# A planned state-space-plus-MLP kernel: raising the rank of the near chunks' exponential, multiplication and mask, with a new draw for the planner

## The chip, the cores and the metric

The kernel runs on one core of a Trainium2 chip. The core has a matrix engine (PE, with its weight loads shown apart as PEld), a vector engine (DVE), an activation engine (ACT), a general engine (POOL) and SP, which issues nearly all DMAs. Each engine works through its own list of instructions in order; semaphores make an instruction wait for another engine or for a DMA. The metric is the device time of one execution in microseconds (us). The kernel before takes 322.32 us (median of 3 runs, 321.84 to 322.35).

## The reference, cut to what matters

```python
# a: (4, 8, 768); x: (4, 8, 768, 32); B, C: (4, 8, 768, 16); chunks of 32 in time
log_a = np.log(np.clip(a, 1e-06, 1.0))
for c in range(nc):
    cum = np.cumsum(la, axis=-1)
    L = np.exp(cum[:, :, :, None] - cum[:, :, None, :])      # decay from j to i
    L = L * causal                                            # i >= j
    M = np.einsum('bhin,bhjn->bhij', Cc, Bc) * L
    y[:, :, sl] = M @ x + (C @ state) * exp(cum)              # written out with einsum
    state = decay_full * state + sum_j decay_from_j * B_j x_j
x = y.transpose(0, 2, 1, 3).reshape(3072, 256)
h = x @ w_in                                                  # 256 x 2048
g = h - np.tanh(h)
return g @ w_out                                              # 2048 x 256
```

A scan over time with a decay for each head comes first; its output feeds a two-layer network with 2048 inner features and `g = h - tanh(h)` between the layers. Both weight matrices arrive as float64.

## The kernel before, in words

**Scan.** The kernel uses chunks of 112 time steps, not 32: 28 chunks, numbered so that the same chunk of the four batches stands together. The 16 rows of state of a batch are put beside the 112 rows of inputs, so that one product of 128 rows does both parts of `y`. For each chunk `ck` there are these steps, whose line numbers are those of the profile:

- the product of B and C (`att`, written on PE), and the decays `exp(cum_i - cum_j)` (`lt`);
- their product with each other on DVE, the causal mask by POOL (`cut`, L547), and then `y` on PE (`y`), which is the masked matrix times x. For chunks that hand a state on, PE also computes the new state (L659 or, for the first pairs of chunks, `z`, L587), and ACT copies it into the top rows of a later x (L593, L665).

The decays are made in three ways. `first_tile` makes chunks 0 to 3: POOL masks a log, PE sums it up (`cp`, L465 and L467), ACT takes the exponential (L482), DVE multiplies (L486). `chunk_a` makes the **near chunks**, 4 to 9: PE makes the sums beside the product of B and C in one `att` buffer (L522, L527), ACT takes the exponential of 128x896 elements (L531), DVE multiplies (L535), POOL masks. `chunk_l` makes the chunks from 10 on: a DMA spreads the sums over the partitions (L560), ACT adds a bias and takes the exponential in eight parts (L565), POOL masks, and `crossed` multiplies on DVE (L699) with an `att` that PE makes for two chunks at once (`cross`, L693). There is one `att` buffer (four banks of PSUM): the next `att` waits until DVE has multiplied with the last. Chunks from 10 on go through PE in pairs (`pair_y`, L719).

**Weights.** `conv(u)` turns a piece `u` of 256 inner features from float64 words (`raw`, loaded by SP at L312, 512 KB for each half: half 0 for the first layer, half 1 for the second) into float32: ACT converts the high words (L341), DVE shifts, clamps and joins bits (L346, L351, L354, L361), and then ACT rounds to the short format (`wh`, L365) and DVE takes the rest (`wl`, L368). Pieces 0 and 1 are done in halves of 128x512 elements, and their plain float32 words are used at once by the first tile (L772 and, from `wf`, L849).

**Network.** The 3072 rows are cut into tiles, four of 256 and four of 512; the four narrow ones are later swept in two pairs, called tiles 8 and 9. For a tile `t` and feature `f`, PE makes `ph{t}_{f}` (L777, three products each of rounded parts and rests; L772 plain), ACT the tanh (L809), DVE the difference `g` (L813), then ACT and DVE split it (`gh` L817, `gl` L823), and PE multiplies by the second layer into `o{t}` (L859, or L849 for pieces 0 and 1 and the narrow tiles). The first sweep covers narrow tiles 0 to 3 with features 0 to 3; a result of it, `o0` to `o3`, is moved away by ACT (L888). The buffers for `ph` are two, and `cp` and the pairs' `y` use the same two. The buffers `po0` and `po1` are one each: `z`, the single chunks' `y` and `o` take turns in them, so that `z1` cannot start before ACT has copied `z0` away.

**What sets the order.** Nothing is issued as it is written. Each step is handed to `op(...)` with its engine, a cost in us and what it reads and writes, and `Order` plans all of them: a list schedule in which an engine, when it is free, takes the ready step of best rank. The rank of a step is its start in a backward schedule, less its `urge`, plus a random number between -0.3 and 0.3:

```python
prio = [-rstart[i] - self.ops[i][1] - self.urge[i] + self.JITTER * rng.uniform(-1, 1) for i in range(n)]
```

A lower number goes first. `search` does 16 rounds from one `SEED` and keeps the plan with the shortest end by its own costs; its order is then issued on all engines, SP included. `URGE` is 3.0 (us). In the kernel before it is given to the steps of `first_tile` for the first tile's chunks (L497, L499, L502) and to the copies of their `y` (L679).

## Time and profile before

| | |
|---|---|
| median of 3 runs | 322.32 us |
| profiled execution, its own time | 322.54 us |
| its span, first to last instruction | 320.8 us |
| what lies around the span | 1.7 us |
| PE busy | 313.0 us, 98% |
| DVE busy | 216.8 us, 68% |
| ACT busy | 210.0 us, 65% |
| POOL busy | 64.1 us, 20% |
| granted PE clock | 0.999 |

A row of a timeline gives the start from the span's beginning and the time taken, then the engine, the line, the operation, and what is written and read; in square brackets stands the idle time of the engine just before it and what ended it. A row of waits gives who waited for what, and the total, the number and the longest in us. Busy times of PE overlap, since a matmul starts before the one ahead has drained; the distance between two starts on PE tells its pace.

### The profile page before, as it was taken

What the parts mean: (1) busy time and instruction counts of PE and PEld (TensorE: products, weight loads), DVE (VectorE), ACT (ScalarE), POOL (GpSimd) and SP (SyncE); (2) the same over time, 40 slices, a digit from 0 to 9 for tenths busy, and PEclk for the clock granted to TensorE, in tenths of its full rate; (3) what the DMA queues carried; (4) which work ended last, traced back from release to release, by engine and by line L of the source; (5) the groups of instructions that cost most, each with busy time, mean ns of one, the idle gap of its engine ahead of it and who ended that gap; (6) DMA issues with size and microseconds to landing.
All of it is one profiled execution on the core that took longest, in us unless ns stands there. A gap on an engine that the chain in (4) does not pass through costs nothing.

```text
span 320.8 us, 5650 instructions
## 1 busy us (share of the span) xinstructions
PE 313.0 (98%) x2112; PEld 251.3 (78%) x2112; DVE 216.8 (68%) x314; ACT 210.0 (65%) x471; POOL 64.1 (20%) x94
## 2 busy tenths in 40 slices
PE   8898999999999999999999999999999999999995
PEld 6466888788888877787878878878878788888883
DVE  7999987798889856558474764574755745645551
ACT  6668888476789679767584773965847744544451
POOL 6525544002223223212120220201101100000000
PEclk9999999999999999999999999999999999999999
DMA  6766686148923256471506005007500000100001
GB/s 199 238 205 251 182 289 252 51 161 246 309 44 66 44 152 160 67 223 38 188 0 225 0 0 210 0 1 233 205 21 0 0 2 0 66 2 0 0 0 65
DMA packets 15450, 35.25 MB, mean 110 GB/s; under 512 B 2464, under 2 KB 4416, under 8 KB 15424
## 3 DMA queue, kind: packets, MB, share of 16 engines
q1 hardware_dynamic: 13696, 31.76, 29.6%
q0 software_dynamic: 1728, 3.15, 5.7%
q8 instruction: 16, 0.26, 0.3%
q14 instruction: 10, 0.08, 0.1%
HBM read 28.32 MB, written 3.43 MB: 99 GB/s over the span
## 4 chain that ended last, share of the span: by engine, by line
PE 89%; DVE 7%; ACT 2%; issue 1%; DVEq 0%; ACTq 0%
PE ph L777 39%; PE o L859 37%; PE o L849 4%; PE y L719 3%; PE att L693 3%; ACT lt L565 1%; DVE lt L486 1%; PE warm L1018 1%; PE y L652 1%; DVE wv L351 1%; DVE wm L354 1%; DVE wm L346 1%; DVE lt L535 1%; DVE wv L361 1%; PE att L527 1%
## 5 line engine op out<-in xcount | busy, mean ns | idle before, releaser
L813 DVE TENSOR_TENSOR g<-ph,g 128x512 f32<-128x512 f32 x96 | 65.9, 687 | 45.7 <-ACT g L809 45.6
L809 ACT ACTIVATE g<-ph 128x512 f32<-128x512 f32 x96 | 57.4, 598 | 56.3 <-PE ph L777 55.3
L823 DVE TENSOR_TENSOR gl<-g,gh 128x512 fp32r<-128x512 f32 x88 | 65.1, 742 | 38.5 <-ACT gh L817 37.3
L777 PE MATMUL ph<-xh,wh 128*128 128x512 f32 (+1 forms) x200 | 75.6, 382 | 0.0
L777 PE MATMUL ph<-xh,wl 128*128 128x512 f32 (+1 forms) x200 | 74.5, 377 | 0.0
L817 ACT CAST gh<-g 128x512 fp32r<-128x512 f32 x88 | 54.3, 618 | 25.6 <-DVE g L813 24.7
L859 PE MATMUL o<-gh,wh 128*128 128x512 f32 x176 | 69.2, 393 | 0.0
L859 PE MATMUL o<-gl,wh 128*128 128x512 f32 x176 | 68.7, 390 | 0.0
L859 PE MATMUL o<-gh,wl 128*128 128x512 f32 x176 | 68.5, 389 | 0.0
L777 PE MATMUL ph<-xl,wh 128*128 128x512 f32 (+1 forms) x200 | 58.0, 376 | 0.0
L547 POOL TENSOR_SCALAR_AFFINE_SELECT lt<-lt 128x896 f32<-128x896 f32 (+1 forms) x24 | 26.8, 1118 | 119.7 <-ACT lt L565 111.6
L777 PEld LDWEIGHTS ph<-xh,wh 128*128 128x128 f32 x200 | 37.6, 188 | 7.8 <-issue 0.7
L777 PEld LDWEIGHTS ph<-xh,wl 128*128 128x128 f32 x200 | 37.6, 188 | 6.8
L777 PEld LDWEIGHTS ph<-xl,wh 128*128 128x128 f32 x200 | 36.3, 188 | 7.0
L565 ACT ACTIVATE lt<-lt,ncum 128x112 f32<-128x112 f32 (+1 forms) x144 | 41.6, 374 | 0.0
L859 PEld LDWEIGHTS o<-gh,wh 128*128 128x128 f32 x176 | 33.0, 188 | 7.7 <-issue 0.8
L859 PEld LDWEIGHTS o<-gl,wh 128*128 128x128 f32 x176 | 33.0, 188 | 7.4 <-DVE gl L823 0.5
L859 PEld LDWEIGHTS o<-gh,wl 128*128 128x128 f32 x176 | 33.0, 188 | 6.7
L904 POOL DMA_DIRECT2D pt<-part x12 | 10.7, 972 | 50.8 <-ACT part L901 50.5
L699 DVE TENSOR_TENSOR lt<-att,lt 128x896 f32<-128x896 f32 (+1 forms) x18 | 18.9, 1050 | 0.0
L849 PE MATMUL o<-g,wf 128*128 128x256 f32 x64 | 15.4, 387 | 0.3 <-DVE g L813 0.3
L849 PEld LDWEIGHTS o<-g,wf 128*128 128x128 f32 x64 | 11.7, 189 | 2.7 <-issue 0.6
(97 smaller groups left out, 266.6 us busy)
## 6 DMA issues: line engine op xcount, KB each, us to landing
lt<-cumr SPq DMA_DIRECT2D x18, 512.0 KB
raw<-w_d SPq DMA_DIRECT2D x16, 512.0 KB
bc<-bc_d SPq DMA_DIRECT2D x14, 352.0 KB
x<-x_d SPq DMA_DIRECT2D x14, 256.0 KB
pt<-part POOLq DMA_DIRECT2D x12, 256.0 KB, 4.1
out_d<-ob SPq DMA_DIRECT2D x8, 256.0 KB
braw<-bn_d SPq DMA_DIRECT2D x14, 112.0 KB
out_d<-pt SPq DMA_DIRECT2D x4, 256.0 KB
```

What stands on the lines that cost most here:

```text
L547: nc.gpsimd.affine_select(out=k["l"][:, :, 0:q], in_=k["l"][:, :, 0:q], pattern=[[0, H], [1, q]], compare_op=ALU.is_ge, fill=0.0, base=N, ...
L565: nc.scalar.activation(k["l"][:, h, 0:q], k["l"][:, h, 0:q], AF.Exp, bias=ncum[:, h, ck : ck + 1])
L693: nc.tensor.matmul(out=a_[:, i], lhsT=bb[r], rhs=cc[r, :, 0 : qlen(ck)], start=True, stop=True)
L699: nc.vector.tensor_tensor(out=l, in0=chs[j]["a"], in1=l, op=ALU.mult)
L777: nc.tensor.matmul(out=ph[:, i * w : i * w + w], lhsT=w_[:, u, 0, k, j * P : (j + 1) * P], rhs=(xh, xl)[p][:, k, ts], start=p == i == k == ...
L809: nc.scalar.activation(g[:, 0:used], gs[t, f][0][:, 0:used], AF.Tanh)
L813: nc.vector.tensor_tensor(out=g, in0=ph, in1=g, op=ALU.subtract)
L817: nc.scalar.copy(gh[:, 0:used], gs[t, f][1][:, 0:used])
L823: nc.vector.tensor_tensor(out=gl[:, 0:used], in0=g[:, 0:used], in1=gh[:, 0:used].bitcast(F32), op=ALU.subtract)
L849: nc.tensor.matmul(out=po[t, seg][e], lhsT=wf[:, u, 256 * j + e * P : 256 * j + (e + 1) * P], rhs=gs[t, f][1][:, i * w : i * w + w], start ...
L859: nc.tensor.matmul(out=po[t, seg][e], lhsT=w_[:, u, 1, j, e * P : (e + 1) * P], rhs=g[:, i * w : i * w + w], start=f == seg[0] and k == 0 ...
L904: op("POOL-", 1.0, lambda e=e: nc.gpsimd.dma_start(out=pts[m][:, e], in_=obs[t, e], accum_op=ALU.add), r=[name, n_pt[2 * m], n_pt[2 * m + ...
```

## The change

Three calls in `chunk_a` (the exponential, the multiplication, the mask of chunks 4 to 9) and the mask of the chunks from 10 on get `urge=URGE`: their rank is improved by 3 us in the plan. The seed of the random part becomes 252 instead of 537. No instruction is added, taken away or altered; the costs that the planner works with are the same.

```diff
-    ROUNDS, JITTER, SEED, EARLY, LOOK = 16, 0.3, 537, 8.0, 0.5
+    ROUNDS, JITTER, SEED, EARLY, LOOK = 16, 0.3, 252, 8.0, 0.5
@@ chunk_a
-        op("ACT", 0.92, fn_e, r=[n_a], w=n_l)
-        op("DVE", 1.08, fn_m, r=[n_a], w=n_l)
-        op("POOL", 0.97, lambda: cut(ck), w=n_l)
+        op("ACT", 0.92, fn_e, r=[n_a], w=n_l, urge=URGE)
+        op("DVE", 1.08, fn_m, r=[n_a], w=n_l, urge=URGE)
+        op("POOL", 0.97, lambda: cut(ck), w=n_l, urge=URGE)
@@ chunk_l
-        op("POOL", 0.97, lambda: cut(ck), w=n_l)
+        op("POOL", 0.97, lambda: cut(ck), w=n_l, urge=URGE)
```

What comes of it is a new order on every engine. In the rows below a name carries the chunk, piece or tile first and a running number last (`wv1_352` is piece 1).

**The loads of weight piece 1, on SP.** Before, from the write-out of the sums (`cum3`) on, up to the second half of `raw1`:

```order
L1067 DMA cum3_115<-parts_111 112x3x128 x2
L312 DMA raw1_208<-w_d 128x1024
L281 DMA bc2_213<-bc_d 128x704
L1072 DMA lt_c_112<-cum3_115 6x1x768
L1074 DMA rt_c_113<-cum3_115 3x2x768
L1072 DMA lt_c_112<-cum3_115 6x1x768
L1074 DMA rt_c_113<-cum3_115 3x2x768
L1072 DMA lt_c_112<-cum3_115 6x1x768
```

Now, from the second of the loads of `rt_c` on:

```order
L1074 DMA rt_c_113<-cum3_115 3x2x768
L1072 DMA lt_c_112<-cum3_115 6x1x768
L1074 DMA rt_c_113<-cum3_115 3x2x768
L1072 DMA lt_c_112<-cum3_115 6x1x768
L1074 DMA rt_c_113<-cum3_115 3x2x768
L312 DMA raw1_284<-w_d 128x1024 x2
L293 DMA x2_348<-x_d 128x512
L302 DMA braw1_107<-bn_d 112x256
```

The first half of `raw1` stood ahead of the eight loads of `lt_c` and `rt_c`, which can only start when the sums have been written out; now both halves stand behind them. (The second half of piece 0 and `bc1`, which stood ahead of the write-out, now stand right behind it.)

**From `att4` to the second feature of tile 0.** On ACT, now, from chunk 4's exponential on:

```order
L531 ACTIVATE lt4_340<-att4_319 128x8x112
L620 CAST xh_91<-y3_331 128x2x112
L341 ACTIVATE wv1_352<-raw1_284 128x512
L632 CAST xh_91<-xf_93 128x2x336
L341 ACTIVATE wv1_352<-raw1_284 128x512
L531 ACTIVATE lt5_389<-att5_358 128x8x112
L593 COPY x2_348<-z0_372 16x2x64 x4
L809 ACTIVATE g0_0_403<-ph0_0_342 128x512
```

On PE, before:

```order
L527 MATMUL att4_343<-bc2_213 128x224 x4
L772 MATMUL ph0_0_354<-xf_93,wv0_192 128x256 x4
L587 MATMUL z0_369<-x0_151,bw0_338 16x32 x16
L772 MATMUL ph0_2_388<-xf_93,wv1_264 128x256 x4
L522 LDWEIGHTS lt_c_112
```

On PE, now:

```order
L522 MATMUL att5_358<-rt_c_113,lt_c_112 128x224
L527 MATMUL att5_358<-bc2_233 128x224 x4
L587 MATMUL z0_372<-x0_164,bw0_218 16x32 x16
L587 MATMUL z1_406<-x1_212,bw1_393 16x32 x16
L772 MATMUL ph0_2_427<-xf_93,wv1_352 128x256 x4
```

`ph0_2` moved from before `att5` and `z1` to behind both; on ACT the copies of `z0` (L593), for which `z1` waits, moved behind both conversions of piece 1 and behind chunk 5's exponential.

**From chunk 7's `y` to `att12`.** On ACT, before, from the rounding of weight piece 2 (`wh`) to the first far exponential, of chunk 10:

```order
L365 CAST wh_89<-wv2_489 128x1024
L620 CAST xh_91<-y7_633 128x2x112
L665 COPY x5_539<-y7_633 16x64 x4
L809 ACTIVATE g2_0_683<-ph2_0_651 128x512
L531 ACTIVATE lt9_690<-att9_674 128x8x112
L341 ACTIVATE wv3_696<-raw3_563 128x1024
L888 COPY pt0_525<-o1_0_0_619 128x2x256
L665 COPY x6_664<-y8_701 16x64 x2
L620 CAST xh_91<-y8_701 128x2x112
L665 COPY x6_664<-y8_701 16x64 x2
L809 ACTIVATE g2_2_746<-ph2_2_721 128x512
L565 ACTIVATE lt10_694<-lt10_694,ncum_105 128x112 x8
```

On ACT, now, to the exponential of chunk 11 (three copies of `y7`, chunk 9's exponential, the cast of `y7` and its last copy stand just ahead of the first row):

```order
L365 CAST wh_89<-wv2_616 128x1024
L341 ACTIVATE wv3_709<-raw3_614 128x1024
L665 COPY x6_666<-y8_713 16x64
L620 CAST xh_91<-y8_713 128x2x112
L665 COPY x6_666<-y8_713 16x64 x3
L809 ACTIVATE g2_0_739<-ph2_0_669 128x512
L809 ACTIVATE g2_2_742<-ph2_2_690 128x512
L565 ACTIVATE lt10_688<-lt10_688,ncum_105 128x112 x8
L665 COPY x6_666<-y9_754 16x64 x3
L620 CAST xh_91<-y9_754 128x2x112
L665 COPY x6_666<-y9_754 16x64
L565 ACTIVATE lt11_730<-lt11_730,ncum_105 128x112 x8
```

On PE, before, from the end of `ph3_2`:

```order
L777 MATMUL ph3_2_824<-xl_92,wh_89 128x256 x4
L849 MATMUL o3_0_0_848<-g3_0_837,wf_94 128x256 x4
L693 MATMUL att12_857<-bc6_786 128x224 x8
L719 MATMUL y10_866<-lt10_694,x5_539 32x128 x8
L719 MATMUL y10_866<-lt11_699,x5_539 32x128 x8
```

On PE, now:

```order
L777 MATMUL ph3_2_827<-xl_92,wh_89 128x256 x4
L693 MATMUL att12_851<-bc6_798 128x224 x8
L719 MATMUL y10_860<-lt10_688,x5_570 32x128 x8
L719 MATMUL y10_860<-lt11_730,x5_570 32x128 x8
L777 MATMUL ph8_4_882<-xh_91,wh_89 128x512
L777 MATMUL ph8_4_882<-xh_91,wl_90 128x512
```

The rounding of piece 2 and the tanh of tile 2 moved behind chunk 7's `y`, and the latter behind chunk 8's copies. On PE the second half of `o1` now stands ahead of `y7` (before, behind it), and the first half of `o3` behind `att12` and the pair's `y` (before, ahead of them); `o1`, `o2` and `o3` are each done in one piece.

## The prediction

> **What bounds the kernel now.** I read the page first, then its chain of waits, then PE's busy time by stretches.
>
> ```profile
> PE 313.0 (98%) x2112; PEld 251.3 (78%) x2112; DVE 216.8 (68%) x314; ACT 210.0 (65%) x471; POOL 64.1 (20%) x94
> ...
> PE   8898999999999999999999999999999999999995
> ...
> PE 89%; DVE 7%; ACT 2%; issue 1%; DVEq 0%; ACTq 0%
> ```
>
> PE is the bound: 98% busy and 89% of the chain that ended last. The digits fall below 9 only in three of the first four slices of 8 us and in the last one. The stretches say the same (columns: PE, PEld, DVE, ACT, POOL busy us, then clock, DMA share, GB/s):
>
> ```profile
> 20.00:30.00 10.00, 8.53 (x155) 6.48 (x152) 9.93 (x16) 8.70 (x19) 4.50 (x5) 1.00 0.91 318
> ...
> 32.06:62.06 30.00, 29.70 (x387) 24.74 (x387) 23.91 (x31) 22.95 (x59) 12.05 (x13) 1.00 0.58 193
> 62.06:110.00 47.94, 47.94 (x213) 39.67 (x212) 42.44 (x56) 36.20 (x68) 10.01 (x13) 1.00 0.52 147
> 110.00:317.00 207.00, 206.95 (x1209) 167.61 (x1207) 120.54 (x176) 128.77 (x299) 25.58 (x36) 1.00 0.23 71
> ```
>
> From 62.06 to 317 us PE is never free for more than 0.05 us in all. The change alters no instruction, so PE has the same matmuls afterwards. Two things follow. What PE gains or loses before 62 us arrives whole at the end, because nothing behind it has slack in which to catch up or be lost. And the gain is limited to PE's waits before 62 us. The two longest are these:
>
> ```profile
> PE att L522 <- DVE lt L535: 1.5, 1, 1.5
> PE att L476 <- DVE lt L486: 0.9, 1, 0.9
> ```
>
> Both are waits for the one `att` buffer, to be freed by a multiplication on DVE. DVE is 9.93 of 10 us busy from 20 to 30 us: the front is DVE's and PE's together, and the masks of POOL, with 4.50 us, have room. I therefore cut the work at two points in PE's list at which both orders have done the same matmuls: the end of `o0` (32.06 us before) and the end of `o3` (62.06 us before).
>
> **Term 1, the front up to the end of `o0`.** The raised rank puts the first chunks' and chunk 4's and 5's multiplications ahead of weight bits on DVE, which attacks the two waits. But the new order also loads weight piece 1 later. These are the rows that price it:
>
> ```profile
> 9.56 0.49 SPq L312 DMA_DIRECT2D raw<-w_d  x1
> 14.48 0.67 ACT L341 ACTIVATE wv<-raw 128x512 f32<-128x512 f32 x1 [0.27 <-DMA raw<-w_d]
> 16.12 0.43 SPq L1074 DMA_DIRECT2D rt_c<-cum  x1
> 16.61 0.34 SPq L302 DMA_DIRECT2D braw<-bn_d  x1
> 18.24 0.68 DVE L361 SCALAR_TENSOR_TENSOR wf<-wv,wm 128x512 uint32<-128x512 uint32 x1
> 19.30 0.64 POOL L404 TENSOR_TENSOR bw<-braw,wdec 128x256 f32<-128x256 f32 x1 [3.22 <-DMA braw<-bn_d]
> 22.73 1.99 PE L772 MATMUL ph<-xf,wv 128*128 128x256 f32 x8
> 23.03 1.05 ACT L593 COPY x<-z 16x128 f32<-16x128 f32 x4
> 24.65 0.27 PE L522 MATMUL att<-rt_c,lt_c 9*128 9x224 bf16 x4
> 25.40 0.92 ACT L531 ACTIVATE lt<-att 128x896 f32<-128x896 f32 x1
> 26.57 1.08 DVE L535 TENSOR_TENSOR lt<-att,lt 128x896 f32<-128x896 f32 x1
> 28.41 3.72 PE L849 MATMUL o<-g,wf 128*128 128x256 f32 x16
> 32.06 0.59 PE L652 MATMUL y<-lt,x 128*32 128x112 f32 x16
> ```
>
> Before, the first half of piece 1 was issued at 9.56 us. Now both halves follow the eight loads of the sums, the last of which goes out at 16.12 for 0.43 us; these loads wait for a write-out that DVE's unchanged first rows release, so I keep the time. The halves go at 16.6 and 17.1. The `braw` load issued at 16.61 was used at 19.30, 2.7 us for 112 KB; 512 KB are 400 KB more, 1.3 us at the 318 GB/s of the stretch from 20 us. The first half lands at 20.6, the second 1.65 us later, at 22.2. ACT, in order, then converts it (0.67) and takes chunk 5's exponential (0.92): 23.8. DVE multiplies (1.08, 24.9) and joins piece 1's bits (0.68, 25.6). ACT copies `z0` (1.05) after the exponential, so that `z1` can start at about 25.0, having held PE since `z0`, some 2 us. `ph0_2` starts at 25.65 and takes 1.92 (22.73 to 24.65): 27.6. What follows it on PE is priced by the chain's rows:
>
> ```profile
> 32.13 0.52 PE y L652 x16
> 32.65 0.12 PE y L659 x16
> 32.77 0.21 PE att L522 x4
> 32.97 0.40 PE att L527 x8
> 33.37 3.07 PE ph L777 x24
> ...
> 37.68 1.93 PE o L849 x8
> ...
> 46.75 1.73 PE o L849 x8
> 48.48 0.97 PE att L693 x16
> ```
>
> `att6` 0.61, `y4` 0.64, `o0` 3.65 (28.41 to 32.06): 32.5. **Term 1 is +0.4 us**: the two old waits are gone, and a new one of about their size stands at `z1` and `ph0_2`. Its bounds: if both halves land after the bare 2.7 us, chunk 5's exponential waits only for ACT's own list, and the term is 0; if the freed DVE brings more, at most the two waits, 2.4 us, are won. On the other side stands the 4.9 us from 9.56 to 14.48, with other loads queued ahead: 17.1 and 4.9 and 1.65 is 23.65, 1.45 later, +1.8.
>
> [...]
>
> **Term 2, from `o0` to `o3`: changes between kinds of work.** The wide matmuls of PE (`ph`, `o`) are done in five runs now instead of seven: `o1` and `o2` are no longer split by small matmuls. A piece of `o` that begins a run takes 1.93 us (37.68), one behind other wide work 1.73 (46.75). Two runs fewer: **-0.4 us**.
>
> **Term 3, the wait for chunk 11's decays.** `att12` needs the `att` buffer, which the multiplication of chunk 11 frees, and now nothing stands ahead of it that PE could do. That multiplication follows chunk 11's mask, and this follows a list on ACT that starts when PE ends `y7`:
>
> ```profile
> 39.11 1.04 ACT L365 CAST wh<-wv 128x1024 fp32r<-128x1024 f32 x1
> 40.44 0.35 ACT L620 CAST xh<-y 128x224 fp32r<-128x224 f32 x1 [0.29 <-PE y L659]
> 40.69 0.85 ACT L665 COPY x<-y 16x64 f32<-16x64 f32 x4
> 41.99 0.60 ACT L809 ACTIVATE g<-ph 128x512 f32<-128x512 f32 x1 [0.45 <-PE ph L777]
> 43.50 1.14 ACT L341 ACTIVATE wv<-raw 128x1024 f32<-128x1024 f32 x1
> 51.32 2.34 ACT L565 ACTIVATE lt<-lt,ncum 128x112 f32<-128x112 f32 x8
> 53.73 0.98 POOL L547 TENSOR_SCALAR_AFFINE_SELECT lt<-lt 128x896 f32<-128x896 f32 x1 [2.14 <-ACT lt L565]
> 54.93 1.08 DVE L699 TENSOR_TENSOR lt<-att,lt 128x896 f32<-128x896 f32 x1
> 55.16 1.97 PE L849 MATMUL o<-g,wf 128*128 128x256 f32 x8 [0.28 <-DVE g L813]
> ```
>
> ACT's list in the new order: copies and cast of `y7`, `y8` and `y9`, each 0.85 and 0.35 (3.60); chunk 9's exponential 0.92; rounding of piece 2 1.04; conversion of piece 3 1.14; two tanh 1.20; chunks 10 and 11, 2.34 each (4.68). That is 12.6 us. With the mask (0.98) and the multiplication (1.08) it is 14.6. PE's work from the end of `y7` to `att12`: `att9` 0.61, `ph2` 3.07, `y8` 0.64, `att10` 0.97, `y9` 0.64, `o2` 3.46, `ph3` 3.07, together 12.5. PE waits 2.2 us with the handovers, at `y9`, `o2` and `att12`. Before, the rounding of piece 2 stood ahead of `y7`, and half of `o1` and of `o3` (1.7 each) stood within this stretch, so PE waited 0.28 us there. **Term 3 is +1.9 us.** What is late next is `o3` and tile 8, and PE is full from there on. Bounds: were mask and multiplication hidden altogether, ACT's 12.6 would still match PE's 12.5, and the term would be -0.2; a mask of twice the time makes it +2.9. I take the rows as they stand, since each operation was measured in this very stretch.
>
> The masks of the far chunks, raised too, cost nothing elsewhere: POOL is 12 of 30 us busy there, and its list has nothing else that PE awaits.
>
> **The sum.** 0.4 - 0.4 + 1.9 = +1.9 us. The profiled execution took 322.5 us, 1.7 more than its span, and would take 324.4; the runs shown have a median of 322.3, 0.2 below it: **324.2 us**, 0.6% slower.
>
> **Rivals.** *The front wins* (0.20, faster). The multiplications ahead of the weight bits remove both old waits (2.4 us), and piece 1 lands early enough that `ph0_2` replaces none of them. For it: DVE was full, and both waits were for it. Against it: SP's order, which sends piece 1 7 us later than before. With term 2 and term 3 unchanged: -2.4 - 0.4 + 1.9 = -0.9, 321.4 us. It decides for faster when `o0` ends before 30 us.
>
> *The ACT list is covered by half* (0.15, no change): PE reaches `y7` by so much waiting elsewhere that ACT is ahead, and only some 0.9 us of term 3 stay. With a front of 0: +0.5, 322.8 us.
>
> *Piece 1 comes much later* (0.12): the 4.9 us of the first load hold for the new ones. 1.8 - 0.4 + 1.9 = +3.3, 325.6 us.
>
> *The clock falls in the new wait* (0.03): if the clock went down and cost half of a warm-up like the first, it would add 1.8 us, 326.0.
>
> ```profile
> 0.85 3.59 PE warm L1018 x16
> ```
>
> *The rank does not do it*: the new draw alone could set this order, and the raised rank nothing. Every number above would stand, so it has no chance of its own; it is a question for runs.
>
> **How the numbers follow.** The forecast as summed has 0.50. With the two slower rivals, slower by over 0.2% (about what a measurement of this kernel can tell, 0.6 us) has 0.65, within 0.2% has 0.15, faster 0.20. The forecast's own range is 323.1 to 325.2, terms 1 and 3 each off by up to 0.8. To leave out no more than 2 in 10, the range goes from 321.4, the winning front, to 325.7, the late piece.
>
> **What would show it.** In the changed kernel's profile: piece 1 issued by SP at about 16.6 us and its second conversion on ACT waiting for a DMA near 22; PE idle some 2 us between `z0` and `ph0_2`, and no longer 1.5 us at `att6`; `o0` ending at 32.5; PE waiting 2.2 us in all between `y7` and `att12`, released by DVE; the end of `o3` near 64, and PE full from there to the last matmul. If `o0` ends by 30 us, term 1 is wrong; if `att12` follows `ph3` at once, term 3 is; if the first two hold and the end does not move, PE has slack behind 62 us that I did not see.

## The result and the profile after

The changed kernel takes **326.71 us** (median of 6 runs, 325.38 to 327.69), the kernel before 322.34 us beside it: a ratio of 1.0134, with a 95% interval from 1.0117 to 1.0150. It is slower, as forecast, but by 4.4 us where 1.9 were forecast, and above the top of the range (325.7). The profiled execution took 327.69 us, the longest of the six, for a span of 326.0, so that again 1.7 us lie around the span. Two executions at a far lower clock (393 us at 0.754 of `urge_only`, 525 us at 0.558 of `decays_first`, both kernels further down) are in the counts and medians below, but not in the ratios.

The page of the changed kernel: the busy times of the engines, PE's busy tenths, the granted clock (the share of PE's full speed that it was given) in tenths, and the chain that ended last.

```profile
PE 315.2 (97%) x2112; PEld 252.7 (78%) x2112; DVE 217.4 (67%) x314; ACT 209.5 (64%) x471; POOL 63.1 (19%) x94
...
PE   8887998899999999999999999999999999999995
...
PEclk9995999999999999999999999999999999999999
...
PE 87%; DMA 4%; DVE 3%; ACT 3%; SPq 1%; issue 1%; POOL 0%; DVEq 0%
```

PE is still the bound, with the same 2112 matmuls, and a DMA has come into the chain. The row to stop at is the third. The fourth slice of 8 us has a 5: for most of 24 to 32 us PE ran at half its clock (0.50 from 25.65 to 32.48 us). No such digit stands in the page of the kernel before, whose mean clock was 0.999. The kernel before is not free of it in every execution, though: of its 65 executions that go into the ratios of the experiments below, 13 show a mean clock of 0.995 or less, and these take 323.4 to 324.5 us.

PE by stretches, cut at the ends of `o0` and `o3` as in the prediction (PE, PEld, DVE, ACT, POOL busy us, then clock, DMA share, GB/s):

```profile
20.00:30.00 10.00, 7.53 (x116) 5.41 (x108) 9.80 (x15) 6.91 (x16) 4.31 (x5) 0.78 0.65 191
...
36.31:67.62 31.31, 29.24 (x388) 24.98 (x387) 26.58 (x34) 24.17 (x61) 9.45 (x11) 1.00 0.65 215
67.62:110.00 42.38, 42.38 (x189) 35.08 (x188) 36.53 (x49) 32.53 (x61) 9.15 (x10) 1.00 0.52 146
110.00:322.00 212.00, 212.00 (x1233) 172.27 (x1231) 124.95 (x181) 131.72 (x305) 27.71 (x37) 1.00 0.23 70
```

The three parts can now be set against the forecast:

| part of PE's list | before | after | change | forecast |
|---|---|---|---|---|
| start to the end of `o0` | 32.06 | 36.31 | +4.25 | +0.4 |
| end of `o0` to the end of `o3` | 30.00 | 31.31 | +1.31 | +1.5 (terms 2 and 3) |
| end of `o3` to PE's last matmul | 254.94 | 254.55 | -0.39 | 0 |

PE is full behind `o3`, as forecast; what a kernel has lost by then it keeps. Nearly all of the error is in the front. These are its rows (start, time taken, instruction, idle time before it and what ended that):

```profile
16.66 0.82 SPq L312 DMA_DIRECT2D raw<-w_d  x2
...
23.59 0.68 ACT L341 ACTIVATE wv<-raw 128x512 f32<-128x512 f32 x1 [0.76 <-DMA raw<-w_d]
24.17 0.90 ACT L531 ACTIVATE lt<-att 128x896 f32<-128x896 f32 x1
24.97 1.05 ACT L593 COPY x<-z 16x128 f32<-16x128 f32 x4
...
23.32 0.43 PE L587 MATMUL z<-x,bw 128*16 128x32 f32 x32
26.12 0.63 PE L587 MATMUL z<-x,bw 128*16 128x32 f32 x32 [2.37 <-ACT x L593]
26.85 3.78 PE L772 MATMUL ph<-xf,wv 128*128 128x256 f32 x8
30.56 0.37 PE L522 MATMUL att<-rt_c,lt_c 9*128 9x224 bf16 x4
...
25.10 1.09 DVE L535 TENSOR_TENSOR lt<-att,lt 128x896 f32<-128x896 f32 x1
26.11 0.68 DVE L361 SCALAR_TENSOR_TENSOR wv<-wv,wm 128x512 uint32<-128x512 uint32 x1
```

The chain is the one in the prediction, link by link: piece 1 issued at 16.66, its second conversion waiting for a DMA, then chunk 5's exponential, `z0`'s copies, `z1`, and on DVE chunk 5's multiplication ahead of the bits that `ph0_2` needs. Two of its numbers are off. The conversion begins at 23.59 and not at 22.2, which puts `ph0_2` at 26.85 and not at 25.65. And from the start of `ph0_2` to the next start on PE it is 3.71 us (26.85 to 30.56), where it was 1.92 before: the half clock (0.50 from 27 to 31 us).

The two waits of the second part are where they were expected, at `y9` and at `att12`:

```profile
52.40 0.59 PE L652 MATMUL y<-lt,x 128*32 128x112 f32 x16 [0.91 <-DVE xl L623]
60.88 1.04 PE L693 MATMUL att<-bc 32*128 32x224 f32 x16 [1.11 <-DVE lt L699]
```

The six runs of the changed kernel tell more than their median, since each has its span and its mean clock: 323.7 us at 1.000, 324.9 at 0.995 (twice), 325.1 and 325.4 at 0.993, and 326.0 at 0.990. The lower the clock, the longer the span, and the one run in which the clock did not fall at all is 2.9 us above the span before. So, from these few runs, some 3 us of the loss come with the order itself, and 0 to 2.3 more with the clock; `warm`, further down, checks that split.

### The profile page after: what moved, and what is told of

The parts are those of the page before. It is cut to its first block, busy times and chain, and to the rows that moved or that the text cites. A ratio compares the mean times of both kernels' runs of the same rounds, so it can differ in the third digit from the quotient of the medians.

```text
span 326.0 us, 5653 instructions
## 1 busy us (share of the span) xinstructions
PE 315.2 (97%) x2112; PEld 252.7 (78%) x2112; DVE 217.4 (67%) x314; ACT 209.5 (64%) x471; POOL 63.1 (19%) x94
## 4 chain that ended last, share of the span: by engine, by line
PE 87%; DMA 4%; DVE 3%; ACT 3%; SPq 1%; issue 1%; POOL 0%; DVEq 0%
PE ph L777 39%; PE o L859 37%; PE o L849 3%; PE y L719 3%; PE att L693 2%; DMA raw<-w_d 2%; DMA x<-x_d 2%; ACT lt L565 1%; PE ph L772 1%; PE y L652 1%; DVE rt_c L1010 1%; PE att L527 1%; ACT x L665 0%; DMA a_sb<-a_d 0%; DVE lt L699 0%
## 5 line engine op out<-in xcount | busy, mean ns | idle before, releaser
L547 POOL TENSOR_SCALAR_AFFINE_SELECT lt<-lt 128x896 f32<-128x896 f32 (+1 forms) x24 | 25.2, 1048 | 131.0 <-ACT lt L565 114.9
L777 PEld LDWEIGHTS ph<-xl,wh 128*128 128x128 f32 x200 | 36.3, 188 | 7.0
```

Source lines behind the costliest of these rows:

```text
L547: nc.gpsimd.affine_select(out=k["l"][:, :, 0:q], in_=k["l"][:, :, 0:q], pattern=[[0, H], [1, q]], compare_op=ALU.is_ge, fill=0.0, base=N, ...
L777: nc.tensor.matmul(out=ph[:, i * w : i * w + w], lhsT=w_[:, u, 0, k, j * P : (j + 1) * P], rhs=(xh, xl)[p][:, k, ts], start=p == i == k == ...
```

## The experiments

Fifteen kernels were run. The first two take the change apart; the others keep a plan and move single steps in it, or put useless work into a gap. For a move, the loop that issues the plan gets a list of pairs; step `i` goes right ahead of step `j`:

```diff
-        for i in sorted(range(n), key=lambda i: (start[i], i)):
+        line = sorted(range(n), key=lambda i: (start[i], i))
+        for i, j in ((35, 65), (37, 65),):
+            line.remove(i)
+            line.insert(line.index(j), i)
+        for i in line:
```

Line numbers in the rows of these kernels are therefore larger by 4 to 10. Ratios are to the kernel before, run on the same chip beside each; "front" ends with `o0`, "second part" with `o3`, both in us from the profiled execution, as is the mean clock. A difference of some tenths in them is not much: `seed_only`, `seed_o3`, `seed_fix` and `seed_mult` have the same order up to `o0`, and their fronts are 31.71 to 30.96.

| run | median us | ratio, 95% interval | front | second part | clock |
|---|---|---|---|---|---|
| changed kernel | 326.71 | 1.0134 (1.0117 to 1.0150) | 36.31 | 31.31 | 0.990 |
| seed_only | 323.70 | 1.0035 (1.0011 to 1.0058) | 31.71 | 31.94 | 0.998 |
| urge_only | 324.59 | 1.0060 (1.0038 to 1.0083) | 33.11 | 30.79 | 1.000 |
| raw_early | 327.65 | 1.0144 (1.0118 to 1.0170) | 36.09 | 31.61 | 0.994 |
| warm | 325.45 | 1.0081 (1.0053 to 1.0108) | 33.72 | 31.39 | 0.998 |
| bits_first | 325.39 | 1.0083 (1.0055 to 1.0110) | 34.55 | 31.45 | 0.992 |
| round_late | 327.79 | 1.0152 (1.0119 to 1.0184) | 36.83 | 31.89 | 0.989 |
| both | 327.19 | 1.0132 (1.0101 to 1.0163) | 34.38 | 32.73 | 0.995 |
| seed_o3 | 324.75 | 1.0060 (1.0037 to 1.0084) | 31.49 | 32.78 | 1.000 |
| copies_late | 326.12 | 1.0115 (1.0089 to 1.0142) | 34.92 | 31.61 | 0.994 |
| warm_bits | 324.56 | 1.0066 (1.0049 to 1.0083) | 33.01 | 31.55 | 0.999 |
| warm_all | 324.28 | 1.0054 (1.0038 to 1.0070) | 32.81 | 31.51 | 0.999 |
| seed_fix | 323.14 | 1.0024 (1.0002 to 1.0045) | 31.32 | 32.07 | 0.998 |
| decays_first | 328.64 | 1.0176 (1.0147 to 1.0205) | 35.95 | 31.86 | 0.993 |
| decays_copies | 327.45 | 1.0155 (1.0128 to 1.0182) | 34.00 | 33.11 | 0.995 |
| seed_mult | 322.37 | 0.9999 (0.9979 to 1.0019) | 30.96 | 31.02 | 1.000 |

### The two halves of the change, each alone

`seed_only` keeps the new draw (252) and takes the raised ranks back; `urge_only` keeps the raised ranks with the old draw (537).

> The new draw (252) without the raised ranks. Its order issues the first half of piece 1 ahead of the sums' loads, as the old order does, and puts ph0_2 ahead of z1; at the other end att12 stands ahead of o3, as in the changed kernel. Theory 'late weights' (the loss in the front comes from piece 1 behind the sums' loads, the rest from the wait for chunk 11's multiplication): the front loses nothing, o0 ends near 31.5-32, the clock stays 1.00 in every run, and only the second part's 1.4 us are lost: 323.2 to 323.8 us. Rival 'the draw makes all of it': 326 to 327 us, like the changed kernel. Rival 'the raised rank makes all of it': 322.3 us, like the kernel before.

> The raised ranks with the old draw (537). Its order has the first half of piece 1 ahead of the sums' loads, ph0_2 ahead of z1, and one half of o3 ahead of att12. Theory 'late weights': neither loss of the changed kernel is there; the sums' loads go out later (behind two more loads), for which I allow 0.5 us: 322.3 to 323.0 us, clock 1.00. Rival 'the raised rank makes all of it': 326 to 327 us. Rival 'the draw makes all of it': 322.3 us; the two draws apart are told by the run with the new draw alone.

Measured: 1.0035 for the draw alone and 1.0060 for the ranks alone, against 1.0134 for both. The draw alone came out in time as the theory said (323.2 to 323.8 us): a front 0.35 us shorter than before, and a second part 1.94 us longer (1.4 were expected), with PE idle ahead of `att12`. One of its twelve executions shows a clock of 0.995, where 1.00 was expected in all.

```profile
56.91 1.04 PE L693 MATMUL att<-bc 32*128 32x224 f32 x16 [1.22 <-issue]
```

The ranks alone were expected at 0 to +0.7 us and cost about 1.9. In their plan `att6` still waits for chunk 5's multiplication, and `o3` waits for its difference, whose tanh stood behind chunk 11's exponential on ACT (53.14 to 55.5):

```profile
28.27 0.28 PE L522 MATMUL att<-rt_c,lt_c 9*128 9x224 bf16 x4 [0.91 <-DVE lt L535]
...
56.98 1.97 PE L849 MATMUL o<-g,wf 128*128 128x256 f32 x8 [1.01 <-DVE g L813]
```

So neither half makes the loss alone. The two add up to 0.95% against 1.34% for the change, a difference that is hardly more than the intervals; and since each of the three is a plan of its own, no sum need hold. Neither of the two plans lets the clock fall in its profiled execution (two other executions of `urge_only` show 0.993); the changed kernel's does. The rival "the raised rank does nothing" falls: with the draw kept, it makes 1.0035 into 1.0134.

### Piece 1 ahead of the sums' loads

`raw_early`: the changed kernel's plan, with the two loads of piece 1 ahead of the eight loads of the sums (the pairs in the diff above).

> The changed kernel's order with one thing moved: the two loads of piece 1 go out ahead of the eight loads of the sums. Theory 'landing and clock': with piece 1 there, ACT goes from xh to the conversion, chunk 5's exponential and z0's copies without its wait for a DMA; z1 starts near 25.4 instead of 26.1, PE's wait there is 1.6 us instead of 2.4, and the clock stays 1.00 in all runs, so that ph0_2 takes 1.9 us and not 3.8. If the landing alone held ph0_2 back, that starts near 25.7 and the time is 324.2 us, my forecast. If DVE's list (chunk 5's multiplication ahead of the joining of piece 1's bits, ready at 25.0) held it back too, ph0_2 still starts near 26.8 and the time is 325.4 us, that of the changed kernel's one run at clock 1.00. Rival 'neither': 326.7 us.

Measured: 1.0144, no gain at all. In number that is the rival "neither", but by a way that nothing in the expectation had. The wait between `z0` and `z1` did shrink, to 1.68 us (1.6 foretold), but `z0` itself came 3.1 us later. Some 1.6 us of this are the sums' loads, which now were late. The rest is the clock, which fell in three of the five runs and in the profiled one at 21.7 us (0.50 from 21.68 to 25.12), so that `ph0_0` took 3.06 us to the next start on PE, where it is 1.92 in the changed kernel. SP's last load of the sums went out at 19.32 and not at 16.17 us, and `att4` waited for it:

```profile
19.32 0.44 SPq L1078 DMA_DIRECT2D rt_c<-cum  x1
...
21.11 0.25 PE L526 MATMUL att<-rt_c,lt_c 9*128 9x224 bf16 x1 [0.35 <-DMA rt_c<-cum]
```

In the two orders tried here, SP's list served the sums or both halves of piece 1 in time, not both. The order of the changed kernel, with piece 1 behind, is not wrong in that; the kernel before and the draw alone send one half ahead and one behind.

### The clock by itself

`warm` fills the wait between `z0` and `z1` with matmuls that nobody needs. They write to the tile that `ph0_2` then overwrites, so nothing else changes:

```diff
+            if G == 1:
+                early[0, 2] = ps_h.tile([P, BANK], F32, tag="ph", name="ph0_2")
+                v = early[0, 2].rearrange("p (h q) -> p h q", h=4)[:, :, 0:Q]
+                for _ in range(12):
+                    nc.tensor.matmul(out=v, lhsT=eye, rhs=never.unsqueeze(1).broadcast_to([P, 4, Q]),
+                                     start=True, stop=True, skip_group_check=True)
             d["z"] = ps_o.tile([P, BANK], F32, tag="po0", name=f"z{G}")
```

> The changed kernel with twelve more matmuls on PE in its wait between z0 and z1 (identity by a constant, bf16, 128 x 448, some 0.19 us each, written to the tile that ph0_2 then overwrites): work that nobody needs, in place of idling. Theory 'clock': the granted clock stays 1.00 in every run, ph0_2 takes 1.9 us though it starts no earlier than 26.8, the spans draw together at 323.7 us, and the time is 325.3 us, 1.2 below the changed kernel's median and 2.3 below its slowest run. Rival 'the low clock is no cause, the runs differ by the landing': spans of 324 to 326 us as before, 326.7 us.

Measured: 325.45 us (325.3 expected) and 1.0081, with a clock of 0.998 or more in all six runs. Their spans did not draw together as expected: they go from 322.4 to 324.6, so a spread of about 2 us is there without the clock. The profiled one is 323.5. PE's rows:

```profile
23.60 2.44 PE L586 MATMUL ph<-never,eye 128*128 128x448 bf16 x12
26.16 0.43 PE L593 MATMUL z<-x,bw 128*16 128x32 f32 x32
26.90 1.99 PE L778 MATMUL ph<-xf,wv 128*128 128x256 f32 x8 [0.30 <-DVE wv L361]
28.82 0.27 PE L522 MATMUL att<-rt_c,lt_c 9*128 9x224 bf16 x4
```

`z1` and `ph0_2` begin when they began before, but `ph0_2` takes 1.92 us to the next start and the front ends at 33.72. In the profiled execution the half clock thus cost 36.31 - 33.72 = 2.6 us, and over the runs 1.0134 - 1.0081 = 0.5%, 1.7 us; the other 0.81%, 2.6 us, is the order. The low clock came from idling: with twelve useless matmuls in the wait the clock is 0.998 or more in all six runs, where it was 0.990 to 0.995 in five of six, and the kernel is faster. The profiles of the later runs that keep the changed kernel's front say the same without useless work. With no half clock in it the front ended at 34.00 (`decays_copies`), with 3.4 us of it at 34.92 and 35.95 (`copies_late`, `decays_first`), and with 6.8 us at 36.31 and 36.83 (the changed kernel, `round_late`).

### The order of the lists in the front

`bits_first` moves two steps of piece 1 and no DMA: on ACT the conversion of the second half behind `z0`'s copies, on DVE the joining of the first half's bits ahead of chunk 5's multiplication.

```diff
+        for i, j in ((168, 184), (165, 209),):
```

> The changed kernel's order with two steps of piece 1 moved and no DMA: on ACT the conversion of its second half goes behind z0's copies (it stood ahead of chunk 5's exponential and waited for the load), on DVE the joining of the first half's bits goes ahead of chunk 5's multiplication (it stood behind). Theory 'order of the lists' (the load may land at 23.6; what hurts is what the lists hold behind it): chunk 5's exponential 23.4 to 24.3, z0's copies to 25.4, z1 at 25.4 after a wait of 1.65 us, the bits joined at 25.7, ph0_2 at 25.9; the clock stays 1.00, as the gap is shorter; o0 ends at 32.8, span 322.5, time 324.2 us. If the clock falls all the same: up to 2.3 more, 326.5. Rival 'the landing is the cause, whatever the lists': 326.7 us.

Measured: runs in two groups, 324.07 to 324.66 (four) and 326.13 to 326.74 (four). These are the two numbers of the expectation, 324.2 with the clock up and 326.5 with the clock down; the clock is 0.998 or more in the lower group and 0.992 to 0.994 in the upper one. The profile is of the upper group:

```profile
25.69 0.52 PE L591 MATMUL z<-x,bw 128*16 128x32 f32 x32 [1.84 <-POOL bw L408]
26.24 3.48 PE L776 MATMUL ph<-xf,wv 128*128 128x256 f32 x8
```

`z1` now waits for POOL, the next in line, and `ph0_2` begins at 26.24, where 25.9 was expected. With a wait of 1.84 us the profiled execution lost its clock (0.50 from 25.87 to 29.28 us); four of the eight, at 0.998 or more, did not. `warm_bits` puts eight useless matmuls into the wait:

> The two steps of piece 1 moved (conversion behind z0's copies, bits ahead of chunk 5's multiplication) and eight of the useless matmuls (1.6 us) in the gap of 1.7 us. The run with the two steps alone gave times in two groups, 324.1 to 324.7 and 326.1 to 326.7, and its profile, of the upper group, shows the clock at half for a part of 24 to 32 us. Theory 'clock': the upper group goes, the clock is 1.00, o0 ends near 33.0, all runs at 324.1 to 324.7 us. Rival 'the two groups have another cause': both groups stay.

Measured: 323.90 to 325.31 us, median 324.56, front 33.01 (33.0 expected), the clock 0.999 or more in all six. The upper group is gone. The two groups were the clock.

### What sets the wait at `att12`

Term 3 blamed ACT's list from `y7` to chunk 11's exponential. `round_late` takes the rounding of piece 2 out of that list (1.04 us on ACT, 1.92 on DVE in the changed kernel) and puts it behind chunk 11.

```diff
+        for i, j in ((262, 343), (263, 337),):
```

> The changed kernel's order with the rounding of piece 2 (1.05 us on ACT, 1.2 on DVE) moved behind the exponential of chunk 11 on ACT and its multiplication on DVE; nothing else. Term 3 as the prediction had it (ACT's list from y7 to chunk 11 is 12.6 us against PE's 12.5): the stretch from the end of o0 to the end of o3, 31.3 us in the changed kernel, gets 1.05 us shorter: 325.6 us. If DVE's list was the limit at y9 too (its low parts waited behind the rounding there), both waits go, up to 2.3 us: 324.4. Rival 'the wait at att12 comes from the mask or from elsewhere': 326.7 us, att12 still waiting 1.1 us. The front is untouched, with its low clock in most runs.

Measured: 1.0152, and a second part of 31.89, not shorter. ACT's and PE's rows:

```profile
51.18 0.20 ACT L669 COPY x<-y 16x64 f32<-16x64 f32 x1 [1.26 <-PE y L663]
```

```profile
52.84 0.59 PE L656 MATMUL y<-lt,x 128*32 128x112 f32 x16 [0.84 <-DVE xl L627]
61.39 1.04 PE L697 MATMUL att<-bc 32*128 32x224 f32 x16 [1.11 <-DVE lt L703]
```

The time that the rounding left free on ACT became a wait of 1.26 us for PE's `y8`. The list that matters does not begin at `y7` but at the end of `y8`, for which ACT itself waits. `both` joins this edit with `bits_first`:

> The two edits before, together: piece 1's conversion and bits moved in the front, piece 2's rounding moved behind chunk 11. If the two parts of the loss add up, as PE's being full behind 62 us says: 324.2 less 1.05 is 323.1 us, or 321.9 if both waits of the second part go. If one of them only gives its gain to the next wait: no better than the better of the two alone.

Measured: 327.19 us, where 321.9 to 323.1 would have been the sum of two gains. The clock fell in five of the six runs (0.990 to 0.995), and the second part is the worse for the rounding, 32.73 us: `att12` waits 1.72. `seed_o3` tries the draw alone with the first half of `o3` ahead of `att12`, as the kernel before has it:

```diff
+        for i, j in ((383, 349),):
```

> The new draw without the raised ranks (323.7 us, 1.0035 of the kernel before), with one matmul group moved: the first half of o3 ahead of att12 on PE, as the kernel before has it. Its second part is 31.9 us long against 30.0 before, with PE idle 1.3 us ahead of att12. Theory 'term 3' (that wait is for chunk 11's multiplication and costs only because nothing stands ahead of att12): the wait goes, one more switch between kinds of work costs 0.2: 322.6 us, the same as the kernel before within 0.2%. Rival 'the wait moves on to o3 or tile 8': 323.7 us.

Measured: 1.0060 (324.75 us, 322.6 expected), a second part of 32.78, longer than the 31.94 without the edit. The wait moved on, as the rival said, to a copy of `o2` on ACT that frees the bank for `o3`:

```profile
56.83 1.99 PE L853 MATMUL o<-g,wf 128*128 128x256 f32 x8 [1.36 <-ACT pt L892]
```

Next, `copies_late` puts `y9`'s four copies behind chunk 11's exponential in the changed kernel:

```diff
+        for i, j in ((306, 343), (307, 343), (308, 343), (309, 343),):
```

> The changed kernel's order with y9's four copies (0.85 us on ACT) moved from ahead of chunk 11's exponential to behind it. Corrected theory of term 3: the list that sets att12 does not begin at y7 (the run with the rounding moved away from there left both waits as they were) but at the end of y8, for which ACT itself waits; from there ACT has y8's copies, two tanh, the exponentials of chunks 10 and 11 and y9's copies and cast, 8.3 us, then mask and multiplication, 10.3, against 8.1 of PE. What is taken out of that piece shortens the wait: chunk 11's exponential 0.85 us earlier, att12 waits 0.4 instead of 1.1-1.3, and from the end of o0 to the end of o3 it is 30.5 us instead of 31.3: 325.9 us with the changed kernel's clock as it falls. Rival 'the mask on POOL or the loads of the decays set it': 31.3 us and 326.7 us as before.

Measured: 326.12 us; the second part is 31.61 where 30.5 was expected, no gain. Now the exponential waited for its own load:

```profile
55.01 2.35 ACT L569 ACTIVATE lt<-lt,ncum 128x112 f32<-128x112 f32 x8 [0.93 <-DMA lt<-cumr]
```

`warm_all` is that edit together with `bits_first` and the useless matmuls:

> The same with y9's copies behind chunk 11's exponential as well. If the front and the second part add up: 0.85 us less than without that edit, 323.4 us, o0 ending near 33.0 and o3 30.5 us later. Rival 'the second part's gain goes into the next wait': 324.3 us.

Measured: 324.28 us; the second part is 31.51 against 31.55 without the edit, so nothing is gained there, and the times of the two, 324.28 and 324.56, lie within each other's intervals.

Two gates, that is, two things that hold chunk 11's exponential, therefore stood within about a microsecond of each other: its load and ACT's list. The last two runs on the changed plan open the other one alone (`decays_first`, the loads of chunks 10 and 11 ahead of an x load and a B load on SP), and then both (`decays_copies`):

```diff
+        for i, j in ((293, 277), (298, 277),):
```

> The changed kernel's order with the loads of chunk 10's and 11's decays moved on SP's list ahead of an x load and a B load that stood before them (issued at 46.9 and 48.5 us there, 12.2 us after the end of o0 for chunk 11; its exponential began 19.8 after it). Two gates were left open for att12's wait: the landing of these loads, and ACT's list (chunk 10's exponential and y9's copies ahead of chunk 11's). Theory 'both gates, the list a little later': the loads land 2 us or more earlier, but chunk 11's exponential still begins 19.8 us after o0, and from the end of o0 to the end of o3 it is 31.3 us as before; 326.7 us. Theory 'the load alone': the wait at att12 goes to 0.3, 30.4 us, 325.8 us.

> The same, and y9's copies behind chunk 11's exponential, an edit that alone gave nothing: the exponential then waited 0.93 us for its load. Theory 'both gates': with both moved, chunk 11's exponential begins some 0.85 us earlier after o0 (near 18.9-19.0), att12 waits about 0.4 us, and from the end of o0 to the end of o3 it is 30.5 us; 325.9 us with the clock as it falls in the changed kernel. Theory 'another gate' (mask, DVE's list): 31.3 us still.

Measured, for `decays_first`: POOL could use both loads at 51.05 (54.87 in the changed kernel), but chunk 11's exponential began 20.3 us after `o0` (19.8 there), and `att12` waited 1.1 us as before. Half a microsecond of that is a side effect: the x load that was passed held up `y8`'s copies and with them `y9`. Counted from the start of `y9`, the exponential began after 3.76 us, against 3.70. The load alone is not the gate:

```profile
56.28 2.34 ACT L569 ACTIVATE lt<-lt,ncum 128x112 f32<-128x112 f32 x8
...
61.06 1.04 PE L697 MATMUL att<-bc 32*128 32x224 f32 x16 [1.11 <-DVE lt L703]
```

For `decays_copies`: with both gates moved, the list of PE's waits has no row for `att12` any more. That by itself proves little, because `o2` ran at half clock here, 5.06 us to the next start instead of 3.39, which alone would cover a wait of 1.1 us. Counted from the start of `y9`, though, chunk 11's multiplication ended after 7.41 us, against 8.22 in the changed kernel and 8.59 and 8.28 with one gate moved: both gates held it, and only the two together let it go, 0.8 us earlier. At full clock some 0.3 us of the wait would be left, an estimate from these rows. And the second part became longer, 33.11 us. The x load that was passed on SP's list is now late for `y8`'s copies on ACT, and `y9` waits twice as long:

```profile
49.68 0.20 ACT L669 COPY x<-y 16x64 f32<-16x64 f32 x1 [1.64 <-DMA x<-x_d]
```

```profile
51.34 0.59 PE L656 MATMUL y<-lt,x 128*32 128x112 f32 x16 [2.12 <-DVE xl L627]
```

In the stretch of 3.41 us around that wait PE was busy for 1.17 us, and in the next one the clock was at half: here, too, an idling PE lost its clock, in a place where the changed kernel kept it (1.00 from 50 to 60 us). The forecast time for this run, 325.9, was missed for these two reasons.

```profile
49.02:52.43 3.41, 1.17 (x39) 0.88 (x34) 2.10 (x5) 2.69 (x10) 0.78 (x2) 1.00 0.99 375
52.43:55.84 3.41, 3.41 (x9) 2.71 (x9) 2.85 (x4) 3.41 (x14) 1.66 (x1) 0.50 0.51 207
```

### Whether the wait can be made to go

`seed_fix` moves `y9`'s copies in the plan of the draw alone, and on DVE the difference for `o1` ahead of a step of piece 2; `seed_mult` moves the copies and puts chunk 11's multiplication ahead of `ph3_0`'s difference on DVE. The pairs of `seed_mult`:

```diff
+        for i, j in ((306, 343), (307, 343), (308, 343), (309, 343), (305, 333),):
```

> The new draw without the raised ranks, with two edits: y9's copies behind chunk 11's exponential (PE idled 1.3 us ahead of att12 there too), and on DVE the difference for o1 ahead of a step of piece 2's bits of 1.9 us, for which PE waited 0.85 us at o1. By the corrected theory the second part goes from 31.9 to 30.1 us, and with its front, 0.35 us shorter than that of the kernel before, it takes 322.0 us, 0.3 less than the kernel before. If only one of the two waits goes: 322.8. Rival 'the waits move on': 323.7 us, as the draw alone.

> The new draw without the raised ranks, with y9's copies behind chunk 11's exponential and that chunk's multiplication ahead of ph3_0's difference on DVE. In the run with the copies alone the mask was done at 54.57 us, but the multiplication stood behind that difference, which waited for PE's own ph3_0, and began at 55.47; att12 still waited 1.0 us. Theory 'each list in turn': with the multiplication ahead, att12 waits 0.3 us or less, from the end of o0 to the end of o3 it is 31.0 us instead of 31.9, and with the front of the draw (0.35 us shorter than before) the time is 322.8 us, level with the kernel before within 0.2%. Rival 'the wait moves to o3, which needs that difference': 31.9 us and 323.7 us.

Measured for `seed_fix`: 1.0024, second part 32.07, no shorter than 31.94 (30.1 expected). The wait of 0.85 us at `o1` went, but one at the start of the second part grew from 0.25 to 1.12, and `att12` still waited 1.02. Chunk 11's mask was ready at 54.57, and these are the two rows of DVE that follow:

```profile
54.86 0.69 DVE L817 TENSOR_TENSOR g<-ph,g 128x512 f32<-128x512 f32 x1 [1.17 <-ACT g L813]
55.47 1.08 DVE L703 TENSOR_TENSOR lt<-att,lt 128x896 f32<-128x896 f32 x1
```

The multiplication stood behind a difference that needed PE's own `ph3_0` first. With the multiplication ahead of it, in `seed_mult`:

```profile
53.93 1.09 DVE L703 TENSOR_TENSOR lt<-att,lt 128x896 f32<-128x896 f32 x1 [1.02 <-POOL lt L551]
```

```profile
55.12 1.04 PE L697 MATMUL att<-bc 32*128 32x224 f32 x16 [0.17 <-PE ph L781]
```

The wait is gone (0.17 us of it is left), the second part is 31.02 us where 31.0 was expected, and the kernel is level with the kernel before, 0.9999 (0.9979 to 1.0019). That is the lowest ratio of all plans tried with the new draw, though its interval still touches that of the draw alone. None of the runs beat the kernel before by more than its interval.

## Why the prediction was right or wrong

**The bound and PE's fullness behind `o3`: right.** In every kernel run PE needs 254.5 to 255.0 us from the end of `o3` to its last matmul, whatever came before, and none got its losses back.

**Term 1, the front: wrong, and this is the step that failed.** It was forecast at +0.4 and came to +4.25 us. The mechanism was the one described, with the two old waits replaced by one at `z1` and `ph0_2`. What failed in it is the landing of piece 1's second half, taken too early, and the clock, which the sum left out. The forecast 0.4, 1.2 us for the later `ph0_2` and 2.6 for the clock make 4.2.

- *The landing of piece 1's second half.* The forecast took 22.2 us, from the nearest row of a small load. ACT began the conversion at 23.59, and the upper bound, worked out from the 4.9 us of the first load, was 23.65. So the right row was that of the same load in the same crowd, not the one of a load of 112 KB. Everything behind it in the chain came as reckoned, and `ph0_2` began 1.2 us late. `bits_first` adds that half of this hangs on the order of the lists: with no load moved, and ACT and DVE doing the other things first, `ph0_2` began 0.6 us earlier.
- *The clock.* "The clock falls in the new wait" was a rival with a chance of 0.03 and a price of 1.8 us. It falls in five of six runs. `warm` prices it at 1.7 us over the runs and 2.6 in the profiled execution, so the price was about right and the chance far too small. Both were the author's estimates: no run shows that a fall costs half of the 3.59 us of the first matmuls, and the chance had one profile behind it, whose clock stayed at 1.00 through a wait of 1.5 us. In the changed kernel a wait of 2.4 us was enough, in a stretch of 3.41 us in which PE was busy for 1.51; and the kernel before itself has a low clock in 13 of 65 executions.

**Terms 2 and 3 together: right in size,** +1.31 against +1.5 us; the two waits are at `y9` and `att12`. Term 2 was not tried by itself, but the stretches shown allow a split. For the same matmuls PE is busy 29.70 us before and 29.24 after, -0.46 where term 2 said -0.4; it is idle 0.30 us before and 2.07 after, +1.77 where term 3 said +1.9.

**Term 3's mechanism: wrong.** The forecast counted ACT's list from the end of `y7` and found 2.2 us of waiting. `round_late` shows that ACT waits for PE again at `y8`, so what stands ahead of that does not count. From the end of `y8` the same rows give, for ACT, `y8`'s and `y9`'s copies and casts (2.4), two tanh (1.2) and two exponentials (4.7), with mask and multiplication 10.3 us; for PE, `att10`, `y9`, `o2` and `ph3`, 8.1. The difference is 2.2 us again: two sums that happened to agree, so that the right size of term 3 is luck. That sum has no load in it, and with ACT's list shortened the load of chunk 11's decays was the next to hold the exponential; `decays_copies` shows that both had to move before chunk 11's multiplication came earlier.

**The rivals.** "The front wins" is out: `o0` ends 4 us later, not earlier. "The ACT list is covered by half" is out: the waits came in full. "Piece 1 comes much later" was true, and with the clock it makes the result: its own number, 325.6 us, lies close to the one run in which the clock did not fall, 325.38. The prediction gave each of two rivals a chance as if only one could hold; they were links of one chain, since the later landing lengthened the wait in which the clock fell. Whether the clock would have kept up with a landing in time is not shown: in `raw_early` it fell at another place. "The seed alone does it" is out as well: `seed_only` and `urge_only` each make a part.

**What would show it.** The issue at 16.66, the idle PE between `z0` and `ph0_2` and PE's fullness behind `o3` were there as announced; the second conversion came at 23.6 and not near 22, `o0` ended at 36.3 and not at 32.5, and `o3` at 67.6 and not near 64.

## What to carry to other kernels

Price a new wait on PE twice, once as the time that it lasts and once with the clock falling in it, which here meant 0.50 for the 3.4 or 6.8 us after it and cost 1.7 us over the runs (`warm`); and price a load that is moved into a crowd by the same load in a crowd (here 4.9 us from issue to use for 512 KB, where a load of 112 KB took 2.7). A sum over an engine's list must begin at the last place where that engine itself waits for the one that is to wait for it. Where several lists are nearly full, moving one step hands the wait to the next list: at full clock, the wait at `att12` went only when every list on its chain gave way (`seed_mult`).

## What the runs showed of the hardware

The stretches of 3.41 us ahead of the fall of the clock, and the time at half clock that followed, of the changed kernel:

```profile
22.24:25.65 3.41, 1.51 (x47) 0.78 (x45) 3.31 (x6) 2.63 (x6) 2.13 (x3) 1.00 0.52 146
25.65:32.48 6.83, 6.26 (x76) 4.35 (x79) 5.63 (x8) 3.80 (x10) 2.18 (x3) 0.50 0.69 201
```

of `bits_first`:

```profile
22.46:25.87 3.41, 1.57 (x70) 0.84 (x73) 3.34 (x6) 2.73 (x7) 2.19 (x3) 1.00 0.45 130
25.87:29.28 3.41, 3.38 (x39) 2.68 (x25) 3.41 (x6) 2.25 (x7) 2.26 (x3) 0.50 0.67 153
```

and of the kernel before, around its longest wait, which kept its clock:

```profile
23.37:26.78 3.41, 2.87 (x83) 2.12 (x82) 3.38 (x7) 3.23 (x8) 2.50 (x3) 1.00 0.99 385
26.78:30.19 3.41, 2.48 (x20) 2.02 (x20) 3.41 (x5) 2.96 (x7) 1.37 (x1) 1.00 0.81 269
```

The half clock lasted 6.83 us in the changed kernel and 3.41 in `bits_first`. In neither was PE idle for the whole stretch ahead of the fall: it was busy for 1.51 and 1.57 us of the 3.41, and its single waits were 2.4 and 1.8 us. In the same stretch ahead of the fall PE was busy for 1.49 us in `copies_late` (24.19 to 27.60 us) and for 1.17 in `decays_copies` (its second part, shown above). The kernel before has 2.87 and 2.48 us in the stretches shown, and 1.94 in the one from 24.30 to 27.71 us, and kept 1.00 in all three. The single wait does not tell it: in `decays_copies` the front had a longer one than either of those two, 2.56 us, and kept its clock; there PE was busy for 2.17 and 1.78 us of the two stretches in which the wait lay:

```profile
26.44 0.43 PE L591 MATMUL z<-x,bw 128*16 128x32 f32 x32 [2.56 <-ACT x L597]
```

```profile
21.71:25.12 3.41, 2.17 (x50) 1.36 (x48) 3.38 (x6) 2.54 (x5) 1.28 (x2) 1.00 0.65 216
25.12:28.53 3.41, 1.78 (x38) 1.56 (x39) 3.14 (x5) 3.13 (x11) 2.69 (x4) 1.00 0.49 129
```

These are a few executions and not a rule. In `raw_early` the clock fell after 3.41 us with 2.33 us busy in short matmuls and waits (18.27 to 21.68), and I can't say why. And `seed_only` has a wait of 2.3 us in its front, yet eleven of its twelve executions show a clock of 0.997 or more. Why the same kernel loses its clock in some executions and not in others, no run shows.
